# Cluster similarities by token: tokens as weights, centroids streamed, parts added by GpSimd, selection spread over four steps

## The chip, the core and the metric

The kernel runs on one core of one Trainium2 chip. TensorE (PE in the profile) does matrix products and writes them to PSUM; its weight loads have rows of their own (PEld). VectorE (DVE), ScalarE (ACT) and GpSimd (POOL) work element by element; SyncE (SP) issues nearly all DMAs. Every engine runs its own instructions in order and waits on semaphores. The metric is the device time of one execution in microseconds (us), lower is better; the time before is the median of three runs.

## The reference, cut to what matters

```
q_n, k_n, c_n = each row divided by its norm
q_assign = argmax(q_n @ c_n.T)      # 16 centroids a head, per token
k_assign = argmax(k_n @ c_n.T)
mask = q_assign[:, None] == k_assign[None, :]
scores = where(mask, scale * q @ k.T, -1e9)
attn = exp(scores - max) / (sum + 1e-9)
x = attn @ v                        # (2 batches x 768 tokens) x 512
h = x @ w_in;  x = (gelu-like of h) @ w_out
h = x @ w_in2; out = (relu(h) ** 2) @ w_out2
```

There are 2 batches, 8 heads, 768 tokens and 64 dimensions a head. The change touches the first three lines, the similarities to 16 centroids and the choice of the largest.

## The kernel before

**Tiles and groups.** Attention works in 8 groups of two heads. A group has 12 query tiles of 128 tokens, so there are 96 tiles in all (`NTILE`). Float32 values are held as two parts, `hi` and `lo` (k1 and k2 for the operand that stacks k in the upper and scaled q in the lower 64 partitions), so that products in the fast float32 format keep their precision.

**The loop.** The main loop runs over t from -2 to 95. A pass issues, in this order: the scores of tile t+2 and their row maximum (`scores`, `rowmax`); six transposes of the exponentials of tile t (`turn_e`, line 426), each half copied by ScalarE (`hi_e`, 436) and its remainder formed by VectorE (`lo_e`, 439); then "mid" and "ahead" side work; a share of the product with the values (`av`, 451; `AV_CUTS` says how many of the 12 matmuls of a block of three tiles fall into each pass); the exponential of tile t+2 (`expo`, 417); and the rest of the side work. Call u = (t+2) mod 12 the step. At step 0 the scores of a new group begin; during steps 0 to 11 the side work prepares the next group. What `side` hands out at each step sets the order; no scheduler moves anything.

**Similarities.** At steps 3 and 4 `sims` takes the centroids `cpad` as weights and streams 384 tokens: four matmuls a step (two heads, k1 and k2). The result has one row per centroid, head and part, so it lies transposed. `simmed` (295) copies it out; at step 5 `best` turns it back with six plain float32 matmuls against a doubled identity, `ident2`, which also adds the two parts (301), into the PSUM bank `pm`.

**Selection.** Still at step 5 `bested` has VectorE take the maximum over 16 and compare (307, 309), and GpSimd weight the hits so that the first one wins (312). At step 7 `hot` takes the maximum and compares again (318, 320), which gives one-hot rows `hot_n`. At step 8 `rows` turns these on TensorE (349), `rowed` has ScalarE turn them into mask values `oh` (359) and issues eight small DMAs (377) that put them under q1 and k1: four for the group's first head, then four for the second. The first scores of the group, at step 12 (step 0 of the next round), read them as 16 more rows of the product (402).

**Beginning and end.** Group 0 has a shorter form of the selection (`first_best`, `first_hot`), head by head on VectorE. After the last tile the first hidden chunk of the first layer is begun (138), in the bank `sd`. That bank was used just before for the last group's sums (`recip_rows`, 485 and 487).

Of the kernel before, what the change touches and what calls it, by code (L numbers as in the profile page):

```python
# [29 lines left out]
def f32(ap):  # L30
    return ap.bitcast(F32)
# [3 lines left out]
def tile_kernel(ctx, tc, q, k, v, cent, w_in1, w_out1, w_in2, w_out2, cw_cols, out):  # L35
# [107 lines left out]
    def attention(actx):  # L143
# [53 lines left out]
        cpad = one.tile([P, H, 2, NS * C], F32R, name="cpad")  # L197
# [13 lines left out]

        ident2 = one.tile([P, NS * C], F32, name="ident2")
        nc.vector.tensor_copy(ident2[0:NS * C], identF[0:NS * C, 0:NS * C])
        nc.vector.tensor_copy(ident2[NS * C:], identF[NS * C:, NS * C:])
# [20 lines left out]
        def centroid_columns(c_hl):  # L235
# [4 lines left out]
            for x in range(2):  # L240
                of = slice(D * (1 - x), D * (2 - x))
                for i in range(G):
                    o = C * (x * G + i)
                    nc.scalar.copy(cpad[of, i::G, :, o:o + C].rearrange("p h t c -> p t h c"),
                                   f32(pc[of, :, i::G, :]))


        class Prep:
# [43 lines left out]
            def simmed(self, half):  # L292
                if half == 0:
                    self.st = one.tile([P, S], F32, tag="st", name="st")
                nc.scalar.copy(self.st[:, half * QB:(half + 1) * QB], self.ps)

            def best(self):

                self.pm = psum([P, NJ, NS, C], F32, "sd", "pm")
                for j in range(NJ):  # L300
                    nc.tensor.matmul(self.pm[:, j].rearrange("p h c -> p (h c)"),  # L301
                                     self.st[:, j * P:(j + 1) * P], ident2, start=True, stop=True)

            def bested(self):
                pm = self.pm
                mx = tiny.tile([P, NJ, NS], F32, tag="mx", name="mx", bufs=1)
                nc.vector.tensor_reduce(out=mx, in_=pm, op=ALU.max, axis=AX)
                sim = one.tile([P, NJ, NS, C], F32, tag="sim", name="sim")
# [3 lines left out]
                nc.gpsimd.tensor_tensor(  # L312
                    out=self.simw.rearrange("p j h c -> p (j h) c"), in0=sim.rearrange("p j h c -> p (j h) c"),
                    in1=cwf.unsqueeze(1).to_broadcast([P, NJ * NS, C]), op=ALU.mult)

            def hot(self):
                fi = tiny.tile([P, NJ, NS], F32, tag="fi", name="fi", bufs=1)
                nc.vector.tensor_reduce(out=fi, in_=self.simw, op=ALU.max, axis=AX)
# [4 lines left out]
            def first_best(self, hh):  # L323

                if not hh:
                    self.sim = one.tile([P, NJ, NS, C], F32, tag="sim", name="sim")
# [3 lines left out]
                pm, sim = self.pm[:, :, hh::G], self.sim[:, :, hh::G]  # L330
                mx = tiny.tile([P, NJ, G], F32, tag="mx1", name="mx", bufs=1)
                nc.vector.tensor_reduce(out=mx, in_=pm, op=ALU.max, axis=AX)
                nc.vector.tensor_tensor(
                    out=sim, in0=pm, in1=mx.unsqueeze(3).to_broadcast([P, NJ, G, C]), op=ALU.is_equal)
# [776 lines left out]
```

## Time and profile before

| | us |
|---|---|
| median of 3 runs | 774.65 (773.09 to 775.04) |
| the profiled execution | 772.62 |
| its span, first to last instruction | 770.8 |
| PE busy | 758.3 (98%) |
| DVE busy | 600.2 (78%) |
| ACT busy | 502.1 (65%) |
| POOL busy | 132.5 (17%) |

The span is 1.8 us shorter than the execution's own time. Attention takes roughly the first third of it, up to 250 us; the two layers take the rest. A busy share tells little about a single stage: what counts is which engine ends last in a step, and that is read in the timelines.

### The profile page before, as it was taken

How to read it: one execution, taken by the hardware profiler on the slowest of the kernel's cores; microseconds unless marked ns; L12 is line 12 of the kernel's file. 1: busy time of each engine (PE TensorE's matmuls, PEld its weight loads, DVE VectorE, ACT ScalarE, POOL GpSimd, SP SyncE). 2: the span in 40 equal slices, each digit the busy share in tenths (PEclk: the TensorE clock that was granted, in tenths of full speed). 3: DMA queues.
4: the chain of work that ended last, by engine and by line, in shares of the span. 5: the costliest groups of instructions: out<-in, count | busy, mean ns of one | idle time of the engine just before them, and what ended most of it. 6: DMA issues, size and time to landing. Idle time of an engine off the chain costs nothing.

```text
span 770.8 us, 12158 instructions
## 1 busy us (share of the span) xinstructions
PE 758.3 (98%) x4400; PEld 694.4 (90%) x4401; DVE 600.2 (78%) x1087; ACT 502.1 (65%) x1035; POOL 132.5 (17%) x151
## 2 busy tenths in 40 slices
PE   7999999999999999999999999999999999999998
PEld 4899999999998899999899999999998888888886
DVE  5899999988898776888888877898778896454532
ACT  5798898898898654544665655576555666445442
POOL 0465474474565100000000000000000000000000
PEclk9999999999999999999999999999999999999999
DMA  9855845734510555445444343314333303100002
GB/s 217 198 122 131 203 106 144 184 90 119 122 42 22 158 172 169 138 151 192 137 149 153 95 129 114 126 45 148 114 121 96 110 28 122 43 28 28 28 1 82
DMA packets 71740, 88.14 MB, mean 114 GB/s; under 512 B 30432, under 2 KB 53760, under 8 KB 71680
## 3 DMA queue, kind: packets, MB, share of 16 engines
q1 hardware_dynamic: 69824, 86.94, 39.4%
q8 instruction: 34, 0.56, 0.3%
q10 hardware_dynamic: 1856, 0.43, 0.3%
q14 instruction: 26, 0.21, 0.1%
HBM read 58.76 MB, written 11.58 MB: 91 GB/s over the span
## 4 chain that ended last, share of the span: by engine, by line
PE 91%; DVE 4%; ACT 1%; DMA 1%; POOL 1%; issue 1%; ACTq 0%; SPq 0%; DVEq 0%; POOLq 0%
PE ps L839 22%; PE y L733 16%; PE y L727 11%; PE pa L451 9%; PE pt L426 8%; PE y L729 6%; PE ph L138 4%; PE ps L402 4%; PE ps L403 4%; PE ps L138 3%; PE pm L301 1%; PE ps L289 1%; PE pt L257 1%; DMA rawkq<-in_q_dram 1%; DVE xl L782 1%
## 5 line engine op out<-in xcount | busy, mean ns | idle before, releaser
L710 ACT ACTIVATE gh<-h 128x384 fp32r<-128x384 f32 (+1 forms) x64 | 41.4, 647 | 101.1 <-DVE h L700 71.2
L408 DVE TENSOR_REDUCE nm<-ps 128x1 f32<-128x768 f32 x96 | 91.6, 954 | 16.6 <-PE ps L403 15.7
L439 DVE TENSOR_TENSOR el<-pt,eh 128x384 fp32r<-128x384 f32 x192 | 97.4, 548 | 5.6 <-ACT eh L436 4.3
L436 ACT CAST eh<-pt 128x384 fp32r<-128x384 f32 x192 | 83.5, 490 | 16.4 <-PE pt L426 16.1
L417 ACT ACTIVATE e<-ps,nm 128x768 f32<-128x768 f32 x96 | 88.1, 917 | 5.8 <-DVE nm L408 5.7
L714 DVE TENSOR_TENSOR gl<-h,gh 128x384 fp32r<-128x384 f32 (+1 forms) x104 | 68.4, 660 | 19.6 <-ACT h L711 19.5
L426 PE MATMUL pt<-identF,e 128*128 128x128 f32 x576 | 80.0, 274 | 0.4 <-DVE el L439 0.4
L733 PE MATMUL y<-ol,gh 128*128 128x512 f32 x192 | 75.9, 395 | 0.1
L733 PE MATMUL y<-oh,gl 128*128 128x512 f32 x192 | 75.9, 395 | 0.0
L733 PE MATMUL y<-oh,gh 128*128 128x512 f32 x192 | 74.7, 389 | 0.0
L402 PE MATMUL ps<-k,q 80*128 80x512 f32 x192 | 69.5, 362 | 0.8 <-ACT k L369 0.8
L426 PEld LDWEIGHTS pt<-identF,e 128*128 128x128 f32 x576 | 65.2, 141 | 2.7 <-DVE el L439 1.9
L403 PE MATMUL ps<-k,q 128*128 128x512 f32 x192 | 62.1, 344 | 0.0
L809 DVE TENSOR_TENSOR wxl<-wb,wxh 128x512 fp32r<-128x512 f32 x37 | 25.6, 691 | 40.7 <-ACT wxh L808 40.7
L727 PE MATMUL y<-gh,ol 128*128 128x512 f32 x128 | 50.0, 391 | 0.0
L727 PE MATMUL y<-gh,oh 128*128 128x512 f32 x128 | 50.0, 391 | 0.0
L727 PE MATMUL y<-gl,oh 128*128 128x512 f32 x128 | 50.0, 391 | 0.0
L839 PE MATMUL ps<-xh,wxh 128*128 128x384 f32 x192 | 48.9, 335 | 0.7 <-DVE h L700 0.7
L839 PE MATMUL ps<-xl,wxh 128*128 128x384 f32 x192 | 49.1, 337 | 0.0
L839 PE MATMUL ps<-xh,wxl 128*128 128x384 f32 x192 | 49.1, 336 | 0.0
L451 PE MATMUL pa<-eh,v 128*128 128x384 f32 x192 | 47.3, 361 | 0.0
L451 PE MATMUL pa<-el,v 128*128 128x384 f32 x192 | 46.6, 352 | 0.0
(198 smaller groups left out, 1882.8 us busy)
## 6 DMA issues: line engine op xcount, KB each, us to landing
raw<-in_moe_w_in_dram SPq DMA_DIRECT2D x32, 512.0 KB, 4.0
raw<-in_moe_w_out_dram SPq DMA_DIRECT2D x32, 512.0 KB, 3.6
wb<-wst SPq DMA_DIRECT2D x24, 512.0 KB, 3.4
q<-k SPq DMA_DIRECT2D x48, 192.0 KB, 3.2
wst<-room SPq DMA_DIRECT2D x16, 256.0 KB, 2.2
wst<-wb SPq DMA_DIRECT2D x13, 256.0 KB, 2.3
rawkq<-in_k_dram SPq DMA_DIRECT2D x16, 192.0 KB, 3.9
k<-k SPq DMA_DIRECT2D x16, 192.0 KB, 5.2
```

What stands on the lines that cost most here:

```text
L402: nc.tensor.matmul(ps[:, a:a + n], q1[0:K1, qs], k1[0:K1, a:a + n], start=True, stop=False)
L403: nc.tensor.matmul(ps[:, a:a + n], q2[:, qs], k2[:, a:a + n], start=False, stop=True)
L408: nc.vector.tensor_reduce(out=nm, in_=live["s", t][:, 0:S], op=ALU.max, axis=AX, negate=True)
L417: nc.scalar.activation(e, live["s", t][:, 0:S], ACTF.Exp, bias=live.pop(("nm", t)), accum_out=sums[:, s:s + 1])
L426: nc.tensor.transpose(pt[:, i], e[:, kc * P:(kc + 1) * P], identF)
L436: nc.scalar.copy(place("eh", t, u), live["pt", t, u])
L439: nc.vector.tensor_tensor(out=place("el", t, u), in0=live.pop(("pt", t, u)), in1=f32(place("eh", t, u)), op=ALU.subtract)
L451: nc.tensor.matmul(pa, v2[:, i % NJ, :], src[:, i % NJ, :], start=(i == 0), stop=(i == 2 * NJ - 1))
L714: nc.vector.tensor_sub(g[1][:, at], h[:, c, at], f32(g[0][:, at]))
L727: nc.tensor.matmul(y[m], l[:, cs], r[:, 0:512], start=first, stop=last)
L733: nc.tensor.matmul(y[m], l[:, m * P:(m + 1) * P], r, start=(begin and z == 0), stop=(fc == KF - 1 and z == 2))
L839: nc.tensor.matmul(ps, w[a][:, wi, kc * P:(kc + 1) * P], x[z][kc], start=start and j == kc == 0, stop=j == 2 and kc == 1, skip_group_check ...
```

## The change

It does seven things.

1. Similarities by token: 128 tokens are the weights and 64 columns of centroids are streamed, so a token's similarities land in its own row. A group has 24 matmuls of 64 columns, 12 at step 3 and 12 at step 4, in the place of 8 of 384 columns; the six plain float32 matmuls and `ident2` are gone. `cpad` is half as wide.
2. The two parts, from the upper and the lower partitions, are added by GpSimd: one addition of 192 elements a partition behind each copy (group 0: by VectorE, from PSUM and a copied part).
3. The selection is one VectorE operation a step: `best` at 5, `bested` at 6, `first` at 7, `hot` at 8. `rows` and `rowed` move from step 8 to step 9.
4. `TURNS`: one of the four transposes of the group after next moves from step 9 to step 8. `AV_CUTS`: four value matmuls a step in three of four blocks.
5. Group 0: its similarities go into the large bank `big0`, so that bank `sd` is free; GpSimd prepares the values of the second head after the splits of group 1 instead of before.
6. The last sums are turned in the spare part of a score bank (`live["s", NTILE - 1]`), not in `sd`.
7. The first hidden chunk: 4 of its 12 matmuls go ahead of the transposes of tile 94, the other 8 ahead of the last value product.

```diff
-            def sims(self, half, tag="sd"):
-                self.ps = psum([P, QB], F32, tag, "ps")
-                cols = slice(half * QB, (half + 1) * QB)
-                both = [(n, hh) for hh in range(G) for n in ("k1", "k2")]
-                for x in both:
-                    nc.tensor.matmul(self.ps, cpad[:, self.h0 + x[1]].rearrange("p t c -> p (t c)"),
-                                     self.__dict__[x][:, cols], start=(x == both[0]), stop=(x == both[-1]))
+            def sims(self, tiles, heads=range(G), ps=None):
+                self.ps = psum([P, NQ, 2, 2, G, C], F32, "sd", "ps") if ps is None else ps
+                for hh in heads:
+                    for i, j in enumerate(tiles):
+                        for n in ("k1", "k2"):
+                            nc.tensor.matmul(self.ps[:, i, :, :, hh], self.__dict__[n, hh][:, j * P:(j + 1) * P],
+                                             cpad[:, self.h0 + hh], start=(n == "k1"), stop=(n == "k2"))
...
-                nc.scalar.copy(self.st[:, half * QB:(half + 1) * QB], self.ps)
+                nc.scalar.copy(st, self.ps.rearrange("p j t x g c -> p j t (x g) c"))
+                nc.gpsimd.tensor_tensor(out=self.sim[:, tiles[0]:tiles[-1] + 1], in0=st[:, :, 0], in1=st[:, :, 1],
+                                        op=ALU.add)
...
-                self.pm = psum([P, NJ, NS, C], F32, "sd", "pm")
-                for j in range(NJ):
-                    nc.tensor.matmul(self.pm[:, j].rearrange("p h c -> p (h c)"),
-                                     self.st[:, j * P:(j + 1) * P], ident2, start=True, stop=True)
+                self.mx = tiny.tile([P, NJ, NS], F32, tag="mx", name="mx", bufs=1)
+                nc.vector.tensor_reduce(out=self.mx, in_=self.sim, op=ALU.max, axis=AX)
...
-                    out=sim, in0=pm, in1=mx.unsqueeze(3).to_broadcast([P, NJ, NS, C]), op=ALU.is_equal)
+                    out=self.sim, in0=self.sim, in1=mx.unsqueeze(3).to_broadcast([P, NJ, NS, C]), op=ALU.is_equal)
...
-            pr = live["s", t][0:GT, S:S + P] if t < NTILE else psum([GT, P], F32, "sd", "pr")
+            pr = live["s", min(t, NTILE - 1)][0:GT, S:S + P]
...
-        AV_CUTS = ((0, 3, 7, 12), (0, 5, 8, 12), (0, 4, 8, 12), (0, 6, 9, 12))
+        AV_CUTS = ((0, 4, 8, 12), (0, 4, 8, 12), (0, 4, 8, 12), (0, 6, 9, 12))
...
-        TURNS = (-5, -3, -1, 0)
+        TURNS = (-5, -4, -1, 0)
...
-            elif u == 8:
-                pe, copy = p.rows, p.rowed
-            if u == 5:
-                ahead, copy = p.best, p.bested
-            if u == 7:
-                mid = p.hot
+            if u == 9:
+                pe.append(p.rows)
+                copy.append(p.rowed)
+            for on, fn in ((5, p.best), (6, p.bested), (7, p.first), (8, p.hot)):
+                if u == on:
+                    mid.append(fn)
...
+            if t == NTILE - 2:
+                first = [hidden(xs, w1, 0, span=slice(0, KD))]
...
-        first = [hidden(xs, w1, 0, span=slice(0, KD))]
+        hidden(xs, w1, 0, first[0], slice(KD, 3 * KD))
...
-        hidden(xs, w1, 0, first[0], slice(KD, 3 * KD))
```

Three places show how the order moves. The first is ScalarE at steps 7 to 9 of the first round, ahead of group 1; `e` is an exponential, `full` the copy for a split, `eh` a copied half of transposes and `oh` the mask values. Before:

```order
L267 ACTIVATE full_582<-pt_574,kq_scale_142 128x384
L436 CAST eh_597<-pt_593 128x3x128
L436 CAST eh_597<-pt_601 128x3x128
L417 ACTIVATE e_613,sums_352<-ps_586,nm_591 128x768
L359 ACTIVATE oh_622<-pf_618,mscale_147 128x384
L436 CAST eh_597<-pt_639 128x3x128
L436 CAST eh_597<-pt_645 128x3x128
L417 ACTIVATE e_654,sums_352<-ps_632,nm_637 128x768
L267 ACTIVATE full_663<-pt_659,kq_scale_142 128x384
```

The same place of ScalarE now:

```order
L260 ACTIVATE full_596<-pt_588,kq_scale_142 128x384
L433 CAST eh_611<-pt_607 128x3x128
L433 CAST eh_611<-pt_615 128x3x128
L414 ACTIVATE e_628,sums_357<-ps_600,nm_605 128x768
L260 ACTIVATE full_637<-pt_633,kq_scale_142 128x384
L433 CAST eh_611<-pt_648 128x3x128
L433 CAST eh_611<-pt_654 128x3x128
L414 ACTIVATE e_664,sums_357<-ps_641,nm_646 128x768
L356 ACTIVATE oh_673<-pf_669,mscale_147 128x384
```

The mask values `oh` and the second `full` have changed places: `oh` comes one exponential later.

The second place is VectorE at steps 5 to 8 of the same round; `mx` and `fi` are the two maxima, `nm` a row maximum of scores and `el` a remainder. Before:

```order
L307 TENSOR_REDUCE mx_510<-pm_495 128x24
L309 TENSOR_TENSOR sim_512<-pm_495,mx_510 128x384
L408 TENSOR_REDUCE nm_521<-ps_516 128x1
L439 TENSOR_TENSOR el_486<-pt_523,eh_485 128x3x128
L439 TENSOR_TENSOR el_486<-pt_529,eh_485 128x3x128
L408 TENSOR_REDUCE nm_546<-ps_541 128x1
L439 TENSOR_TENSOR el_486<-pt_548,eh_485 128x3x128
L439 TENSOR_TENSOR el_486<-pt_554,eh_485 128x3x128
L318 TENSOR_REDUCE fi_560<-simw_514 128x24
L320 TENSOR_TENSOR hot_n_562<-simw_514,fi_560 128x384
L408 TENSOR_REDUCE nm_591<-ps_586 128x1
```

The same place of VectorE now, from the second operation of the selection on:

```order
L300 TENSOR_TENSOR sim_459<-sim_459,mx_519 128x384
L405 TENSOR_REDUCE nm_563<-ps_558 128x1
L436 TENSOR_TENSOR el_510<-pt_565,eh_509 128x3x128
L436 TENSOR_TENSOR el_510<-pt_571,eh_509 128x3x128
L309 TENSOR_REDUCE fi_577<-simw_550 128x24
L405 TENSOR_REDUCE nm_605<-ps_600 128x1
L436 TENSOR_TENSOR el_612<-pt_607,eh_611 128x3x128
L436 TENSOR_TENSOR el_612<-pt_615,eh_611 128x3x128
L314 TENSOR_TENSOR hot_n_621<-simw_550,fi_577 128x384
L405 TENSOR_REDUCE nm_646<-ps_641 128x1
```

Two pairs have become four single operations, and the last of them stands one row maximum later.

The third place is TensorE at the end of attention; `pr` and the last `ps` are the turned sums, `ph` the first hidden chunk. Before:

```order
L451 MATMUL pa<-eh,v_3344 128x384 x4
L426 MATMUL pt<-identF,e 128x128 x6
L451 MATMUL pa<-eh,v_3344 128x384 x2
L451 MATMUL pa<-el,v_3344 128x384 x6
L426 MATMUL pt<-identF,e 128x128 x6
L485 MATMUL pr<-identF,sums 12x128
L138 MATMUL ph<-xh,wi 128x384 x4
L451 MATMUL pa<-eh,v_3344 128x384 x6
L451 MATMUL pa<-el,v_3344 128x384 x6
L138 MATMUL ph<-xl,wi 128x384 x4
```

The same place of TensorE now:

```order
L448 MATMUL pa<-eh,v_3412 128x384 x4
L138 MATMUL ph<-xh,wi 128x384 x4
L423 MATMUL pt<-identF,e 128x128 x6
L448 MATMUL pa<-eh,v_3412 128x384 x2
L448 MATMUL pa<-el,v_3412 128x384 x6
L423 MATMUL pt<-identF,e 128x128 x6
L482 MATMUL ps<-identF,sums 12x128
L138 MATMUL ph<-xl,wi 128x384 x4
L138 MATMUL ph<-xh,wi 128x384 x4
L448 MATMUL pa<-eh,v_3412 128x384 x6
```

Four matmuls of the hidden chunk moved ahead of the transposes of tile 94 and eight ahead of the last value product.

## Rows read from the trace of the kernel before

**Rows 1.** The page: busy time by engine; the chain that ended last, by engine.

```profile
PE 758.3 (98%) x4400; PEld 694.4 (90%) x4401; DVE 600.2 (78%) x1087; ACT 502.1 (65%) x1035; POOL 132.5 (17%) x151
PE 91%; DVE 4%; ACT 1%; DMA 1%; POOL 1%; issue 1%; ACTq 0%; SPq 0%; DVEq 0%; POOLq 0%
```

**Rows 2.** Timeline, TensorE, steps 4 and 5: start, length, line, tiles, count.

```profile
27.89 0.94 PE L289 MATMUL ps<-k,cpad 128*128 128x384 f32 x4
28.67 0.40 PE L402 MATMUL ps<-k,q 80*128 80x512 f32 x1
...
29.15 0.28 PE L402 MATMUL ps<-k,q 80*128 80x256 f32 x1
29.27 0.28 PE L403 MATMUL ps<-k,q 128*128 128x256 f32 x1
29.39 0.82 PE L426 MATMUL pt<-identF,e 128*128 128x128 f32 x6
30.05 1.52 PE L301 MATMUL pm<-ident,st 128*128 128x64 f32 x12
31.38 0.78 PE L451 MATMUL pa<-eh,v 128*128 128x384 f32 x3
```

**Rows 3.** Timeline, TensorE, a later round, end of step 8 to step 12.

```profile
68.42 0.34 PE L349 MATMUL pf<-identB,hot_n 128*128 128x128 bf16 x3
68.58 0.48 PE L402 MATMUL ps<-k,q 80*128 80x512 f32 x1
...
70.79 0.48 PE L402 MATMUL ps<-k,q 80*128 80x512 f32 x1
...
72.93 0.39 PE L402 MATMUL ps<-k,q 80*128 80x512 f32 x1
...
75.25 0.48 PE L402 MATMUL ps<-k,q 80*128 80x512 f32 x1
```

**Rows 4.** Timeline, ScalarE, the same round, steps 8 and 9.

```profile
69.44 0.71 ACT L359 ACTIVATE oh<-pf,mscale 128x384 fp32r<-128x384 bf16 x1
...
71.61 0.65 ACT L267 ACTIVATE full<-pt,kq_scale 128x384 f32<-128x384 f32 x1
```

**Rows 5.** Timeline, SyncE's queue, the same round.

```profile
70.17 1.34 SPq L377 DMA_DIRECT2D q<-oh  x2
71.56 1.22 SPq L377 DMA_DIRECT2D k<-oh  x2
```

**Rows 6.** The one-hot DMAs of that round (line 377): issue to landing.

```profile
DMA to landing us min/median/max: 1.9/1.9/1.9
```

**Rows 7.** Timeline, VectorE, the same round, steps 7 to 9.

```profile
66.90 0.56 DVE L320 TENSOR_TENSOR hot_n<-simw,fi 128x384 bf16<-128x384 f32 x1
...
68.34 1.02 DVE L439 TENSOR_TENSOR el<-pt,eh 128x384 fp32r<-128x384 f32 x2
69.57 0.96 DVE L408 TENSOR_REDUCE nm<-ps 128x1 f32<-128x768 f32 x1 [0.20 <-PE ps L403]
```

**Rows 8.** Timeline, GpSimd, the same round.

```profile
68.59 1.02 POOL L269 TENSOR_TENSOR k<-full,k 128x384 fp32r<-128x384 f32 x1
69.69 1.01 POOL L474 TENSOR_TENSOR x<-both 64x384 f32<-64x384 f32 x1
```

**Rows 9.** Timeline, VectorE and GpSimd around 85 us.

```profile
85.29 1.01 POOL L474 TENSOR_TENSOR x<-both 64x384 f32<-64x384 f32 x1 [2.87 <-DMA both<-both]
85.40 1.45 DVE L100 SCALAR_TENSOR_TENSOR raw<-raw,raw 128x512 uint32<-128x512 uint32 x1
```

**Rows 10.** VectorE's line 100 in attention: duration ns min/median/max, first and last start.

```profile
L100 DVE SCALAR_TENSOR_TENSOR raw<-raw,raw x4: 674/1109/1450, 56.0 to 144.6; 128x512 uint32<-128x512 uint32 x4
```

**Rows 11.** Timeline, TensorE and ScalarE, end of attention.

```profile
247.66 1.01 PE L426 MATMUL pt<-identF,e 128*128 128x128 f32 x6 [0.41 <-DVE el L439]
...
251.88 0.25 ACT L487 COPY rows<-pr 12x128 f32<-12x128 f32 x1
...
252.27 0.93 PE L138 MATMUL ph<-xh,wi 128*128 128x384 f32 x4 [1.44 <-POOL x L474]
```

**Rows 12.** Timeline, TensorE, group 0: its one-hot rows are turned.

```profile
15.78 0.34 PE L349 MATMUL pf<-identB,hot_n 128*128 128x128 bf16 x3 [1.01 <-DVE sim L333]
```

More of the change, by code (lines that the diff above doesn't have):

```diff
@@ L196, in attention @@
         nc.vector.memset(kq_scale[D:], SCALE)
-        cpad = one.tile([P, H, 2, NS * C], F32R, name="cpad")
+        cpad = one.tile([P, H, 2, 2, C], F32R, name="cpad")
         nc.vector.memset(f32(cpad), 0.0)
@@ L241, in centroid_columns @@
                 of = slice(D * (1 - x), D * (2 - x))
[L242 to L245, printed above, removed]
+                nc.scalar.copy(cpad[of, :, :, x].rearrange("p h t c -> p t h c"), f32(pc[of]))
         class Prep:
@@ new lines, in simmed @@
+            def simmed(self, tiles):
+                if not tiles[0]:
+                    self.st = one.tile([P, NJ, 2, NS, C], F32, tag="st", name="st")
+                    self.sim = one.tile([P, NJ, NS, C], F32, tag="sim", name="sim")
+                st = self.st[:, tiles[0]:tiles[-1] + 1]
+                nc.scalar.copy(st, self.ps.rearrange("p j t x g c -> p j t (x g) c"))
+                nc.gpsimd.tensor_tensor(out=self.sim[:, tiles[0]:tiles[-1] + 1], in0=st[:, :, 0], in1=st[:, :, 1],
+                                        op=ALU.add)
@@ L306, in bested @@
[L306 to L308 removed]
+                mx = self.mx
                 nc.vector.tensor_tensor(
[L310 removed]
+                    out=self.sim, in0=self.sim, in1=mx.unsqueeze(3).to_broadcast([P, NJ, NS, C]), op=ALU.is_equal)
@@ L325, in first_best @@
                 if not hh:
+                    self.st = one.tile([P, NJ, 2, NS, C], F32, tag="st", name="st")
                     self.sim = one.tile([P, NJ, NS, C], F32, tag="sim", name="sim")
@@ L519, in attention @@
         w1 = (wi[:, 0, :], wi[:, 1, :]) + out_tiles(0)
-        for half in range(2):
-            p0.sims(half, ("sd", "pa")[half])
-            p0.simmed(half)
+        p0.sims(range(NJ), ps=psum([P, 8, 2, 2, G, C], F32, "big0", "ps"))
         nc.scalar.activation(tiny.tile([P, 1], F32, name="warm", bufs=1), identF[:, 0:1], ACTF.Exp)
@@ L528, in attention @@
         raw = [w_dma(w_in1, 0, True, 0), w_dma(w_out1, 0, False, 1)]
-        p0.best()
         p0.first_best(0)
         p0.first_hot(0)
-        for i in range(2):
-            p0.vals(i)
+        p0.vals(0)
         tags = iter(("pt0", "pt1", "pa", "big1"))
@@ L550, in attention @@
         dec = raw_tile(2).rearrange("p n t -> p (n t)")
-        none = lambda: None
-        TURNS = (-5, -3, -1, 0)
+        TURNS = (-5, -4, -1, 0)
         def side(gn, u):
-            mid = ahead = spare = pe = copy = none
+            mid, spare, pe, copy = [], [], [], []
             if not 0 < gn < NG:
-                return mid, ahead, spare, pe, copy
+                return mid, spare, pe, copy
             p = ops.get(gn) or Prep(gn)
@@ L563, in side @@
                 hh, half = divmod(TURNS.index(u), 2)
[L564 to L578 removed]
+                pe.append(lambda: p.turn(hh, half))
+                copy.append(lambda: p.split(hh, half))
+            if u in (3, 4):
+                at = range((u - 3) * NQ, (u - 3 + 1) * NQ)
+                pe.append(lambda: p.sims(at))
+                copy.append(lambda: p.simmed(at))
+            if u == 9:
[4 more added lines that the diff above has]
+                    mid.append(fn)
+            if u in (-2, 1) and gn > 1 or gn == 1 and u in (2, 3):
+                spare.append(lambda: p.moved(u in (1, 3)))
+            if u in (8, 8 + 1):
+                spare.append(lambda: p.vals(u - 8))
+            if u == 4 + 1:
+                spare.append(lambda: [p.joined(hh) for hh in range(G)])
             if u in (1, 2, 3) and gn + 1 < NG:
                 load(gn + 1, (0, 1, "v")[u - 1])
[L581 removed]
+            return mid, spare, pe, copy
         for t in range(-LEAD, NTILE):
@@ L601, in attention @@
             for fns in now:
-                fns[0]()
-            for fns in now:
-                fns[1]()
+                for fn in fns[0]:
+                    fn()
             if blk > 0 and t < NTILE - 1:
@@ L617, in attention @@
                 expo(t + LEAD)
-            for fns in list(zip(*now))[2:]:
-                for fn in fns:
+            for part_fns in list(zip(*now))[1:]:
+                for fn in sum(part_fns, []):
                     fn()
```

37 lines of the change are left out of this document (13 added, 24 removed).

## The prediction

> **What bounds the kernel.** I read the page first: TensorE is busy 758.3 of 770.8 us, and 91% of the chain that ended last is TensorE's [rows 1]. Then the timelines of single steps, to see whether TensorE's order has holes that a change can fill or open. Inside attention there are almost none: matmul follows matmul. So a change there counts in two ways only: work taken off TensorE's order, and waits that open in it. Work moved between the other engines counts only where it makes TensorE wait. I write step u for the passes of one round, 0 to 11; step 12 is step 0 of the next round. Seven rounds prepare a group (groups 1 to 7); group 0 is prepared ahead of the loop.
>
> **1. The similarity matmuls.** Before, a group has 4 matmuls of 384 columns at step 3 and 4 at step 4. The four at step 4 take from 27.89 to the next start at 28.67, 0.78 us [rows 2]. The six plain float32 matmuls at step 5 have two records each: 12 records from 30.05 to 31.38, 1.33 us, 0.111 each [rows 2]. A group costs 2 x 0.78 + 1.33 = 2.89 us. After, it has 24 matmuls, each with a new load of 128 x 128 weights and 64 columns. No row before shows this one. The nearest is the record of the six plain matmuls, with the same load size and the same 64 columns, at 0.111; the transposes with their 128 x 128 loads pace the same, six from 29.39 to 30.05, 0.11 each [rows 2]. That makes 24 x 0.111 = 2.66, a gain of 0.23 a group. From above: the shortest matmul of this number format has 256 columns and takes 0.12, from 29.15 to 29.27 [rows 2]; if 64 columns are no cheaper, 24 x 0.12 = 2.88 and nothing is gained. From below: the three bf16 transposes take 68.58 - 68.42 = 0.16, 0.053 each [rows 3]; 24 x 0.053 = 1.28, a gain of 1.6. I stay with the row that has the same loads, halfway to the upper one: 0.12 a group, 8 x 0.12 = **-1.0**. The point is that the loads set the pace, so that streaming six times fewer columns frees almost nothing.
>
> A page of the Trainium skill says otherwise: TensorE: Matmul & The Clock Gate, section on the back-to-back issue gap, gives about 81 ns per pair of load and matmul at 128 columns. The trace shows 110 ns for such pairs with float32 weights [rows 2]. By the page a group would cost 1.94 us, the term would be -7.6, and the sum below 772.1 in place of 778.7; it is taken up as a rival, priced there from rows.
>
> **2. The mask rows come a step later.** This is the largest term. In the round shown, ScalarE starts the mask values at 69.44 and ends 0.71 later [rows 4]; the first DMAs issue at 70.17, the second pair at 71.56, so the fourth at about 72.17 [rows 5]; 1.9 us later it has landed [rows 6], at 74.1. The first scores of the new group start at 75.25 [rows 3]. They read the rows of the first head's q and of all its k, so they wait for the fourth DMA. Margin before: about 1.15 us. After, `rows` and `rowed` stand at step 9: the mask values take the place where ScalarE now does a split copy, at 71.61 [rows 4]. That is 2.17 later; TensorE's distance from there to step 12 does not grow (the step 9 that had three transposes has the three one-hot ones in their place, and steps 10 and 11 keep their four value matmuls). The fourth DMA then lands at about 76.25, **1.0 us after** TensorE needs it. Behind that one matmul queue all of TensorE's next scores, transposes and value products; VectorE and ScalarE only run dry, so nothing is won back. Bounds: 0.7, if part of the 1.9 is not waited for or TensorE is itself a little later; 1.3, if the mask values start later still (part 3). I take 0.95, seven times: **+6.6**.
>
> SyncE's other DMAs behind these eight (the merge copy, the q and k of the group after next) move 2 us too; their readers come three or more steps later, so I cost them at nothing; if that margin were gone, a step would wait as here.
>
> **3. One selection operation a step.** Same four operations, other places. VectorE's regular work in a step is 0.96 + 1.02 = 1.98 us, and it waits only 0.20 for the next scores [rows 7]; a step of TensorE with four value matmuls takes 72.93 - 70.79 = 2.14, and 2.32 with three transposes more [rows 3]. Each selection operation adds 0.56 [rows 7]. Steps 5 to 8 now need 4 x 2.54 = 10.2 us of VectorE against 2 x 2.14 + 2 x 2.32 = 8.9 of TensorE, since the six plain matmuls that made step 5 long are gone and steps 3 and 4 hold the similarity work. The 1.2 us of backlog is partly absorbed by the idle time before it and worked off in steps 9 to 11. What is left makes TensorE wait for a free transpose bank or a late exponential. On top, `hot` moves to a time when GpSimd is at work: before, it started at 66.90, ahead of GpSimd's 68.59 [rows 7, 8]; now it starts near 69.4, between 68.59 + 1.02 and an operation at 69.69 [rows 8]. A VectorE operation with two inputs in the main on-chip memory waits for a GpSimd one: line 100 takes 0.67 alone and 1.45 when it starts 0.11 after a GpSimd addition [rows 9, 10]. So `hot` can cost up to 0.8 more. Bounds a round: 0 (all absorbed) and 1.3. I take 0.4, the part of the backlog that steps 9 to 11 can't take: 7 x 0.4 = **+2.8**.
>
> **4. GpSimd's additions.** 14 of 192 elements, at most 1.0 each (the 384-element one takes 1.02 [rows 8]). ScalarE's copy ends early in step 5 and VectorE reaches the maximum only after its 1.98 of regular work, so they are covered; uncovered, up to 1 us a round. GpSimd is busy 17% [rows 1]. ScalarE's copies stay as long. Cost 0.
>
> **5. The end of attention.** TensorE waits 0.41 before the transposes of tile 94 and 1.44 before the hidden chunk [rows 11]. The second wait ends with ScalarE's copy of the turned sums, 251.88 + 0.25, since both use bank `sd` (the row names a GpSimd operation that ended at the same time; the chunk needs none that late). After, the sums lie in a score bank, four matmuls of the chunk fill the first wait and eight the second; a group of four takes 0.77 with its start-up, so both waits fill. What follows, ScalarE's split of the next weights, comes forward with the value product. **-1.9**, between -1.0 and -2.3.
>
> **6. Start.** The turn of group 0's one-hot rows waited 1.01 us for VectorE's second-head comparison, since both shared `sd` [rows 12]. That bank is now free, but one addition and one copy are new in the chain. I take **-0.4**, between -1.0 and +0.7.
>
> **Sum.** -1.0 + 6.6 + 2.8 - 1.9 - 0.4 = +6.1. Against the profiled execution's own 772.6 that gives 778.7; the median of the runs lies 2.0 above that execution, so the median after should be **780.7 us**.
>
> **Rivals.**
> - *The mask rows land in time, VectorE's backlog is absorbed.* Then only the gains remain: -1.0 - 1.9 - 0.4 = -3.3, **771.4 us, faster**. It decides where the fourth DMA's landing falls against the first score matmul of step 12: from a margin at or above zero there the kernel is faster. Against it: the move is a whole step of 2.17 and the margin 1.15. For it: I read the margin in one round, and only one execution.
> - *Half of it.* Waits at their lower ends, 7 x 0.7 = +4.9 and no backlog: +1.6, **776.2**, no difference that can be told.
> - *Loads pace faster than I read.* At the bf16 pace the gain is 1.6 a group, 12.9 in all in place of 1.0: 780.7 - 11.9 = **768.8**. For: the columns are few. Against: every pair with 128 x 128 float32 weights paces at 0.11. The skill's 81 ns lies between and would give 774.1.
> - *The small products cost two records each*, as the plain float32 ones do: 48 x 0.111 = 5.33 against 2.89, +2.4 a group, 8 x 2.4 = +19.5 in place of -1.0: **801**. Against: the 384-column ones of this format have one record each.
>
> **How the numbers follow.** A measurement of this kernel can tell about 0.3%, 2.3 us: faster is below 772.3, slower above 777.0. Forecast (mask rows late, 776.5 to 787 by the bounds of parts 2 and 3): 0.55, all slower. In time: 0.22, of which 0.18 faster, 0.04 same. Half of it: 0.12, of which 0.07 same, 0.04 slower, 0.01 faster. Faster loads: 0.08, of which 0.05 faster, 0.03 same. Two records: 0.03, slower. Sums: faster 0.24, same 0.14, slower 0.62. The range for 8 in 10 goes from 770.8, just below the in-time case, to 786.5; the forecast's own range is 776.5 to 787.
>
> **What would show it.** In the profile after: at step 12 of each round, the first score matmul with idle time of about 1 us released by a DMA of the mask rows, seven times, 6 to 7 us in all (part 2). At steps 6 to 9, transposes or scores waiting for VectorE's remainders, and `hot` longer than 0.56 beside GpSimd (part 3). The 24 small matmuls at 0.11 each, one record each (part 1). No wait of 1.44 before the hidden chunk (part 5). I am wrong if the step-12 matmuls show no DMA wait, or if the small matmuls pace well under 0.1.

## The result: 779.2 us, slower

| | before | after |
|---|---|---|
| median of the runs taken together, us | 773.87 (772.58 to 775.04, 4 runs) | 779.21 (778.95 to 779.37, 4 runs) |
| span of the profiled execution, us | 770.8 | 777.6 |
| PE busy, us | 758.3 | 758.7 |
| DVE busy, us | 600.2 | 597.9 |
| POOL busy, us | 132.5 | 141.8 |

The ratio is 1.0069, 95% interval 1.005 to 1.0088: slower by 5.3 us, where the forecast sum was +6.1. The time lies in the range and the sign is right. The sum behind it is less right: its largest term came out too small, and the second largest was not there at all.

The page of the changed kernel, busy time by engine and the chain that ended last by engine, answers to [rows 1]:

```profile
PE 758.7 (98%) x4432; PEld 693.8 (89%) x4433; DVE 597.9 (77%) x1087; ACT 504.6 (65%) x1033; POOL 141.8 (18%) x165
...
PE 83%; DVE 7%; ACT 4%; DMA 2%; issue 2%; SPq 1%; ACTq 0%; DVEq 0%
```

TensorE does as much as before in a span 6.8 us longer: the loss is waiting, and TensorE's share of the chain falls from 91% to 83%. What it waits for stands in the table of waits of the changed kernel (engine, waiting instruction, what released it: us in total, times, longest):

```profile
PE ps L399 <- DMA k<-oh: 5.5, 5, 1.5
PE ps L399 <- ACT full L260: 2.3, 2, 1.2
PE pt L423 <- DVE el L436: 0.2, 1, 0.2
```

Line 399 is the first score matmul, and the seven waits are those of step 12. One of them, in the timelines of TensorE, SyncE's queue and ScalarE, the round of [rows 3 to 5]:

```profile
73.97 0.39 PE L399 MATMUL ps<-k,q 80*128 80x512 f32 x1
...
75.34 0.94 PE L448 MATMUL pa<-eh,v 128*128 128x384 f32 x4
76.12 0.49 PE L250 MATMUL pt<-identF,rawkq 128*128 128x128 f32 x3
77.77 0.47 PE L399 MATMUL ps<-k,q 80*128 80x512 f32 x1 [1.16 <-ACT full L260]
```

```profile
73.58 1.34 SPq L374 DMA_DIRECT2D q<-oh  x2
74.97 1.22 SPq L374 DMA_DIRECT2D k<-oh  x2
```

```profile
72.89 0.66 ACT L356 ACTIVATE oh<-pf,mscale 128x384 fp32r<-128x384 bf16 x1
...
77.10 0.61 ACT L260 ACTIVATE full<-pt,kq_scale 128x384 f32<-128x384 f32 x1
```

The row puts this wait down to `full`, a ScalarE copy that happens to end at 77.71, but the first scores need nothing of it; the fourth mask DMA, issued at about 74.97 + 0.61 = 75.58, is 2.2 us old when TensorE goes on (the run kfirst below settles which of the two it is). Idle time in a row is counted from the modelled end of the last matmul. I count from first score matmul to first score matmul instead: step 11 lasts 77.77 - 73.97 = 3.80 here, and 75.25 - 72.93 = 2.32 before [rows 3], with the same instructions. In the seven rounds it lasts 3.63 to 3.79 (before 2.07 to 2.42), together **9.9 us** more.

The same reckoning for other steps shows where an experiment loses or gains, so it stands here once for all. Lengths of steps 5 to 11 in us, median of the seven rounds, each the distance between the starts of two first score matmuls:

| step | before | after | rows8 | hot7 | kfirst | pair5 | halves | oldcuts |
|---|---|---|---|---|---|---|---|---|
| 5 | 3.32 | 2.15 | 2.16 | 2.15 | 2.15 | 2.16 | 2.16 | 1.98 |
| 6 | 2.09 | 2.07 | 2.06 | 2.07 | 2.07 | 2.06 | 2.07 | 2.08 |
| 7 | 2.49 | 2.31 | 2.31 | 2.31 | 2.31 | 2.90 | 2.37 | 2.65 |
| 8 | 2.47 | 2.40 | 2.30 | 2.40 | 2.40 | 2.30 | 2.31 | 2.49 |
| 9 | 2.21 | 2.30 | 2.79 | 2.61 | 2.30 | 2.39 | 2.67 | 2.27 |
| 10 | 2.14 | 2.17 | 2.15 | 2.16 | 2.16 | 2.16 | 2.16 | 2.16 |
| 11 | 2.32 | 3.69 | 2.31 | 3.47 | 3.03 | 2.31 | 2.31 | 2.31 |

### The profile page after: what moved, and what is told of

Read it like the earlier page. It is cut to its first block, busy times and chain, and to the rows that moved or that the text cites. A ratio compares the mean times of both kernels' runs of the same rounds, so it can differ in the third digit from the quotient of the medians.

```text
span 777.6 us, 12239 instructions
## 1 busy us (share of the span) xinstructions
PE 758.7 (98%) x4432; PEld 693.8 (89%) x4433; DVE 597.9 (77%) x1087; ACT 504.6 (65%) x1033; POOL 141.8 (18%) x165
## 4 chain that ended last, share of the span: by engine, by line
PE 83%; DVE 7%; ACT 4%; DMA 2%; issue 2%; SPq 1%; ACTq 0%; DVEq 0%
PE ps L835 21%; PE y L729 16%; PE y L723 11%; PE pa L448 6%; PE pt L423 6%; PE y L725 6%; PE ph L138 4%; PE ps L399 4%; PE ps L138 3%; PE ps L400 3%; PE ps L282 2%; DVE el L436 1%; ACT e L414 1%; DVE nm L405 1%; DMA k<-oh 1%
## 5 line engine op out<-in xcount | busy, mean ns | idle before, releaser
L399 PEld LDWEIGHTS ps<-k,q 80*128 80x128 f32 x192 | 36.7, 191 | 15.5 <-ACT e L414 8.0
```

What stands on the lines that cost most here:

```text
L399: nc.tensor.matmul(ps[:, a:a + n], q1[0:K1, qs], k1[0:K1, a:a + n], start=True, stop=False)
```

## The experiments

Theory A: the loss is the wait for the mask DMAs and nothing else. Theory B: the similarities by token or the additions on GpSimd cost something. Theory C, from my forecast: one selection operation a step gives VectorE a backlog for which TensorE pays. Medians are compared with runs of the kernel before on the same chip, 772.9 us in each of the four sets that follow. The changed kernel was not run again in these sets (its own kernel before stood at 773.87), so a difference to it of about 1 us is read from the table of steps and not from the medians.

**rows8: the mask rows a step earlier again.**

```
-        TURNS = (-5, -4, -1, 0)
+        TURNS = (-5, -3, -1, 0)
-            if u == 9:
+            if u == 8:
                 pe.append(p.rows)
...
-            for on, fn in ((5, p.best), (6, p.bested), (7, p.first), (8, p.hot)):
+            for on, fn in ((5, p.best), (6, p.bested), (7, p.first), (7, p.hot)):
```

> The changed kernel with the mask rows (rows, rowed) back at step 8, the one-hot rows (hot) at step 7 behind first, and the four transposes of the group after next back at their old steps; everything else as changed. Theory A (the whole loss is TensorE waiting at step 12 for the fourth mask DMA): the seven waits, 8.9 us together in the changed kernel's trace, are gone, so 779.2 - 8.9 = 770.3 us, 3.6 below the kernel before (ratio 0.995), and no step-12 score matmul shows idle time. Theory B (the similarities by token or the additions on GpSimd cost something that the trace puts down to the mask rows): part of the 8.9 stays, 773 us or more. Theory C (my forecast's term for VectorE's backlog): two operations at step 7 make TensorE wait at steps 7 to 8, visible as idle time there.

771.46 us, ratio to the kernel before 0.9975 (0.9966 to 0.9984): 7.7 us less than the changed kernel. Step 11 is back at 2.31. The rest of the change, without the late mask rows, makes the kernel faster, so B, which asked for 773 or more, falls. But 1.2 us of the expected 8.9 are missing (9.9 by step 11), and the table shows where: step 9 lasts 2.79. It has the three float32 transposes now (71.30 - 71.06 = 0.24) where the changed kernel has the bf16 ones (0.15), which makes 2.39, and pair5 below, with the same matmuls in step 9 and no wait there, has just 2.39. The other 0.40 is a wait of the transposes, in two halves. TensorE's rows there and its weight loads' rows (PEld), which name the releaser:

```profile
69.19 0.28 PE L400 MATMUL ps<-k,q 128*128 128x256 f32 x1
69.50 0.31 PEld L423 LDWEIGHTS pt<-identF,e 128*128 128x128 f32 x3 [0.24 <-DVE el L436]
69.50 1.01 PE L423 MATMUL pt<-identF,e 128*128 128x128 f32 x6
69.96 0.31 PEld L423 LDWEIGHTS pt<-identF,e 128*128 128x128 f32 x3 [0.16 <-DVE el L436]
71.06 0.49 PE L250 MATMUL pt<-identF,rawkq 128*128 128x128 f32 x3
71.30 0.48 PE L399 MATMUL ps<-k,q 80*128 80x512 f32 x1
```

The transposes need a bank that VectorE's remainder `el` (line 436) has yet to read, and VectorE is late: `first` and `hot` stand in one step, behind a delay from steps 5 and 6 (the table under oldcuts).

**hot7: that pair alone.** The mask rows stay at step 9; only `hot` goes to step 7.

```
-            for on, fn in ((5, p.best), (6, p.bested), (7, p.first), (8, p.hot)):
+            for on, fn in ((5, p.best), (6, p.bested), (7, p.first), (7, p.hot)):
```

> The changed kernel with hot at step 7 behind first, ahead of GpSimd's operations, and the mask rows left at step 9. Theory A: hot is only a small part of why the mask values are late (it holds up the row maximum of step 9 and with it the exponential ahead of the mask values by about 0.1 us), so the seven waits fall by at most 0.15 each: 778.2 to 779.2 us. Theory C (one selection operation a step costs by itself, 0.4 us a round as forecast): 776.4 us.

780.23 us, 1.0 **slower** than the changed kernel. Both expectations missed, and C most of all. `hot` takes 0.56 there in place of 0.73, and the step-11 wait shrinks by 0.2 (3.69 to 3.47), but step 9 grows by 0.31 (2.30 to 2.61), again a wait of the transposes for `el`. The first score matmul of step 8 and VectorE's timeline of hot7:

```profile
67.38 0.48 PE L399 MATMUL ps<-k,q 80*128 80x512 f32 x1
68.17 0.54 DVE L309 TENSOR_REDUCE fi<-simw 128x24 f32<-128x384 f32 x1
68.74 0.56 DVE L314 TENSOR_TENSOR hot_n<-simw,fi 128x384 bf16<-128x384 f32 x1
69.22 0.95 DVE L405 TENSOR_REDUCE nm<-ps 128x1 f32<-128x768 f32 x1
70.08 1.01 DVE L436 TENSOR_TENSOR el<-pt,eh 128x384 fp32r<-128x384 f32 x2
```

The same step of the changed kernel:

```profile
67.11 0.48 PE L399 MATMUL ps<-k,q 80*128 80x512 f32 x1
68.34 0.95 DVE L405 TENSOR_REDUCE nm<-ps 128x1 f32<-128x768 f32 x1
```

The row maximum of step 8 starts 69.22 - 67.38 = 1.84 into its step, in the changed kernel 68.34 - 67.11 = 1.23: 0.61 later. So the pair is what costs here. One operation a step costs TensorE nothing: step 6 lasts 2.07 (before 2.09); step 7 is 0.18 shorter, which is the value matmul of 0.17 that left it; step 8, where a value matmul left and the three transposes grew from 0.16 to 0.25, is 0.07 shorter.

**kfirst: another order of the DMAs.**

```
                 for hh in heads:
-                    for x in range(2):
-                        for z in range(2):
-                            dst, src = piece(x, hh, z)
-                            nc.sync.dma_start(f32(dst), f32(src))
+                    for x, z in ((0, 0), (1, 0), (1, 1), (0, 1)):
+                        dst, src = piece(x, hh, z)
+                        nc.sync.dma_start(f32(dst), f32(src))
```

> The changed kernel with one thing moved: of the four DMAs of a head, the two for k stand ahead of the second one for q, which only the odd query tiles read. Nothing moves on TensorE, ScalarE or VectorE. Theory A: the last DMA that step 12 needs is now the third, issued 0.63 us earlier, so each of the seven waits falls from 1.28 to about 0.65 us: 779.2 - 4.4 = 774.8 us. If the wait is for something else (the score bank, ScalarE's copy that ends at the same time in the record): 779.2, no change.

774.53 us, ratio 1.0019 (1.001 to 1.0027): 4.7 less than the changed kernel, 4.4 expected. Step 11 falls by 0.66 to 3.03. No compute engine's order moved, so this is the run that shows theory A: TensorE waits for the last DMA that its first score matmul reads. TensorE and SyncE's queue:

```profile
74.41 0.49 PE L250 MATMUL pt<-identF,rawkq 128*128 128x128 f32 x3
75.27 0.47 PE L398 MATMUL ps<-k,q 80*128 80x512 f32 x1 [0.36 <-issue]
```

```profile
71.87 0.67 SPq L373 DMA_DIRECT2D q<-oh  x1
72.59 1.25 SPq L373 DMA_DIRECT2D k<-oh  x2
```

The third DMA, the second of k's, issues at about 73.2, and TensorE starts 2.0 to 2.1 later, as it does behind the fourth in the changed kernel.

**tailback: the end of attention as before.**

```
-            pr = live["s", min(t, NTILE - 1)][0:GT, S:S + P]
+            pr = live["s", t][0:GT, S:S + P] if t < NTILE else psum([GT, P], F32, "sd", "pr")
...
-            if t == NTILE - 2:
-                first = [hidden(xs, w1, 0, span=slice(0, KD))]
...
-        hidden(xs, w1, 0, first[0], slice(KD, 3 * KD))
+        first = [hidden(xs, w1, 0, span=slice(0, KD))]
...
         merged(blk, nc.vector)
+        hidden(xs, w1, 0, first[0], slice(KD, 3 * KD))
```

> The changed kernel with the end of attention as before: the last sums turned in bank sd, the first hidden chunk begun behind the turned sums. Theory: the end's two waits of 0.41 and 1.44 come back, 779.2 + 1.9 to 2.3 = 781.1 to 781.5 us. Rival (the next stage absorbs it, so that the change's gain at the end is not real): 779.2.

781.5 us, 2.3 more than the changed kernel. The two waits of [rows 11] come back at the same size, 0.41 and 1.44. The gain at the end is real, and nothing after it takes it back.

**before_rows9: the move alone, in the old kernel.**

```
-        TURNS = (-5, -3, -1, 0)
+        TURNS = (-5, -4, -1, 0)
...
-            elif u == 8:
+            elif u == 9:
                 pe, copy = p.rows, p.rowed
```

> The kernel before with one part of the change alone: the mask rows (rows, rowed) at step 9 and, to free their bank, the transpose of the group after next from step 9 to step 8. Old similarities, selection in pairs, old end. Theory A: in the trace of before the first scores start 3.05 us after the fourth mask DMA's issue; in the changed kernel they could not start earlier than 2.0 to 2.15 after it; a step of 2.2 later leaves 0.85 of distance, so each of seven rounds waits about 1.2: +8.4, 773.0 + 8.4 = 781.4 us. Theory B (the new similarities or GpSimd's additions make the changed kernel's waits): no change, 773 us.

783.27 us, ratio 1.0131 (1.0116 to 1.0146): 10.3 more than before, 8.4 expected. The waits of step 12 are there without any of the new similarities. TensorE, one of them:

```profile
78.61 0.49 PE L257 MATMUL pt<-identF,rawkq 128*128 128x128 f32 x3
80.11 0.47 PE L402 MATMUL ps<-k,q 80*128 80x512 f32 x1 [1.01 <-DMA k<-oh]
```

Step 11 is 9.1 us longer in seven rounds together. The remaining 1.2 was not followed further; in the profiled execution group 1's similarities also wait 1.3 us for GpSimd's splits.

**pair5: the pair at another step.** On top of rows8:

```
-            for on, fn in ((5, p.best), (6, p.bested), (7, p.first), (7, p.hot)):
+            for on, fn in ((5, p.best), (5, p.bested), (6, p.first), (7, p.hot)):
```

> The changed kernel with the mask rows at step 8 (as in the run with rows and rowed back at step 8), and the selection one step earlier instead of a pair at step 7: best and bested at step 5, first at 6, hot at 7. Theory: the run with the pair at step 7 has a wait of 0.2 us a round, TensorE's transposes of step 9 waiting for a remainder of VectorE, 1.4 us in seven rounds; at step 5 VectorE has just stood idle for the two long similarity steps, so the pair costs nothing there: 771.5 - 1.4 = 770.1 us, with no wait at all in the seven rounds. Rival (the pair costs the same wherever it stands): 771.5, with waits at step 6 or 7.

773.1 us, 1.6 more than rows8 and no better than the kernel before (1.0002, 0.9993 to 1.0011). My theory falls: the idle time that VectorE had ahead of step 5 is no use to a pair at step 5, since the pair comes behind that step's row maximum and remainders. Step 7 grows from 2.31 to 2.90 and step 9 gives back 0.40, 0.2 a round net. TensorE's timeline:

```profile
64.06 0.28 PE L400 MATMUL ps<-k,q 128*128 128x256 f32 x1
64.56 1.01 PE L423 MATMUL pt<-identF,e 128*128 128x128 f32 x6 [0.23 <-DVE el L436]
```

**halves: the selection in halves**, begun at step 4, so that step 7 holds half of `first` beside `hot` (on top of rows8; `best`, `bested` and `first` take a half z of three tiles):

```
...
+            for on, fn, z in ((4, p.best, 0), (5, p.best, 1), (5, p.bested, 0), (6, p.bested, 1), (6, p.first, 0),
+                              (7, p.first, 1)):
+                if u == on:
+                    mid.append(lambda fn=fn, z=z: fn(z))
+            if u == 7:
+                mid.append(p.hot)
...
```

> The changed kernel with the mask rows at step 8, the one-hot rows at step 7 and the transposes at their old steps (as the run with rows and rowed back at step 8), and the selection's first three operations cut in halves of three tiles each, begun a step earlier: maximum of the first half at step 4; maximum of the second and comparison of the first half at 5; comparison of the second and first-hit maximum of the first at 6; first-hit maximum of the second half and the whole hot at 7. Theory (a step holds one VectorE operation of 0.56 more without loss; what exceeds it makes TensorE's transposes wait for a free bank): step 7 now has 0.3 + 0.56 in place of 1.12 and the wait of 0.2 a round shrinks to nothing: 771.5 - 1.4 = 770.1 us. Rival (small operations cost nearly as much as whole ones, and GpSimd's two half products collide with VectorE's): 771.5 or more.

772.4 us, 0.9 more than rows8. Step 9 falls by 0.12, but steps 7 and 8 grow by 0.07 together, so six rounds gain little. In the trace a half operation of three tiles takes 0.33 to 0.35 us (one `bested` half 0.50), where a whole one takes 0.54 to 0.56, so two halves cost VectorE more than the whole. The seventh round loses 1 us: `hot` runs into a long GpSimd operation. GpSimd, VectorE and TensorE there:

```profile
215.22 1.83 POOL L505 TENSOR_TENSOR x<-x,rr 128x768 f32<-128x768 f32 x1
```

```profile
215.72 1.75 DVE L320 TENSOR_TENSOR hot_n<-simw,fi 128x384 bf16<-128x384 f32 x1
```

```profile
217.52 0.34 PE L352 MATMUL pf<-identB,hot_n 128*128 128x128 bf16 x3 [0.80 <-DVE hot_n L320]
```

**oldcuts: the old shares of the value product.** On top of rows8:

```
-        AV_CUTS = ((0, 4, 8, 12), (0, 4, 8, 12), (0, 4, 8, 12), (0, 6, 9, 12))
+        AV_CUTS = ((0, 3, 7, 12), (0, 5, 8, 12), (0, 4, 8, 12), (0, 6, 9, 12))
```

> The changed kernel with the mask rows at step 8 and the pair first, hot at step 7 (as the run with rows and rowed back at step 8), and the old shares of the value product: five matmuls at steps 7 and 8 in place of four, fewer at steps 5 and 9. Theory: the pair at step 7 costs 0.3 us a round only because steps 7 and 8 are 0.17 shorter each on TensorE than in the kernel before, where the same pair at step 7 cost nothing; with the old shares VectorE has that time back, and the step-9 wait goes: 771.5 - 7 x 0.3 = 769.4 us. Rival (the wait comes from elsewhere, as from GpSimd's and ScalarE's order at step 8): 771.5.

771.13 us, ratio 0.9973 (0.9962 to 0.9984), not told apart from rows8: 0.3 less, 2.1 expected. Step 9 falls to 2.27, by 0.17 for the matmul that moved and by 0.35 for the wait; step 7 grows by 0.34, twice the 0.17 of the matmul that came. Half of the wait has only moved forward by two steps.

Why the kernel before bears its pair at step 7 can be read from VectorE's timelines. From the start of one row maximum to the next, VectorE needs 1.80 to 1.85 us in a step without a selection operation (where it has no idle time), 2.26 with one and 2.85 with two. Here are the row maxima of steps 6 to 8 of the changed kernel, then those of steps 7 and 8, with the pair in between, of the kernel before and of rows8:

```profile
63.83 0.95 DVE L405 TENSOR_REDUCE nm<-ps 128x1 f32<-128x768 f32 x1
...
66.09 0.95 DVE L405 TENSOR_REDUCE nm<-ps 128x1 f32<-128x768 f32 x1
...
68.34 0.95 DVE L405 TENSOR_REDUCE nm<-ps 128x1 f32<-128x768 f32 x1
```

```profile
64.52 0.96 DVE L408 TENSOR_REDUCE nm<-ps 128x1 f32<-128x768 f32 x1 [0.18 <-PE ps L403]
...
67.38 0.95 DVE L408 TENSOR_REDUCE nm<-ps 128x1 f32<-128x768 f32 x1
```

```profile
65.19 0.95 DVE L405 TENSOR_REDUCE nm<-ps 128x1 f32<-128x768 f32 x1
...
68.03 0.95 DVE L405 TENSOR_REDUCE nm<-ps 128x1 f32<-128x768 f32 x1
```

The pair costs VectorE the same in both; what differs is how long the step is and how late VectorE already is. The table gives the start of the row maximum behind the start of its step's last score matmul (us, median of six rounds; 0.32 where VectorE has been waiting for the scores). A wait of TensorE in the next step, if there is one, stands in brackets:

| step | before | after | rows8 | pair5 | oldcuts |
|---|---|---|---|---|---|
| 6 | 0.32 | 0.51 | 0.52 | 1.11 (0.59) | 0.69 (0.17) |
| 7 | 0.32 | 0.70 | 0.71 | 1.30 | 0.88 |
| 8 | 0.60 | 0.56 | 1.16 (0.40) | 0.57 | 0.99 (0.05) |
| 9 | 0.32 | 0.77 | 0.65 | 0.32 | 0.32 |

Before, step 6 holds no operation and step 7 lasts 2.49, so the pair starts on time and leaves VectorE 0.28 late, which TensorE does not notice. With one operation in each of steps 5 and 6, the pair comes on top of 0.39 (rows8, where step 7 lasts 2.31) or 0.56 (oldcuts). In pair5 the pair starts on time, but its step lasts only 2.16, and VectorE is 0.79 late behind it. No run changes the delay ahead of the pair alone.

**rows8_kfirst: a control.** rows8 with the DMA order of kfirst.

> A control: the changed kernel with the mask rows at step 8, and k's mask DMAs ahead of q's second one. Theory: where the fourth DMA is in time, its place costs nothing and gains nothing: the same as with the rows at step 8 alone, 771.5 us.

771.09 us (0.9975, 0.9964 to 0.9986), the same as rows8: where nothing waits for the DMA, its place is worth nothing.

**rows10: the mask rows later still.**

```
-            if u == 9:
+            if u == 10:
                 pe.append(p.rows)
```

> The changed kernel with the mask rows one step later still, at step 10. Theory A: each of the seven waits at step 12 grows by the length of a step, 2.15 to 2.2 us: 779.2 + 7 x 2.2 = 794.5 us. Rival (ScalarE's order absorbs part of it, since no split copy stands at step 10): less than 790.

824.5 us, 45 more than the changed kernel, not 15. Step 11 lasts 8.7 in the middle rounds. The mask values end on ScalarE at 81.51 + 0.67 = 82.2, but their DMAs now stand in SyncE's order behind three that move the next group's q (line 271), and those issue from 82.94 on:

```profile
82.94 1.74 SPq L271 DMA_DIRECT2D q<-k  x3
84.79 1.42 SPq L374 DMA_DIRECT2D q<-oh  x2
```

So a step of 2.2 is paid, and then 2.6 more in the queue. Step 0 behind the wait lasts 4.33 in the place of 2.38, and the seven together 13.4 us more: that is TensorE's clock, in the last section.

**halfcols: half the columns**, in groups 1 to 7. It leaves out the product with the low part of the centroids.

```
+                            out, c = self.ps[:, i, :, :, hh], cpad[:, self.h0 + hh]
+                            if self.gi:
+                                out, c = self.ps[:, i, 0, :, hh], cpad[:, self.h0 + hh, 0]
-                            nc.tensor.matmul(self.ps[:, i, :, :, hh], self.__dict__[n, hh][:, j * P:(j + 1) * P],
-                                             cpad[:, self.h0 + hh], start=(n == "k1"), stop=(n == "k2"))
+                            nc.tensor.matmul(out, self.__dict__[n, hh][:, j * P:(j + 1) * P],
+                                             c, start=(n == "k1"), stop=(n == "k2"))
...
```

> The changed kernel with half the columns in the 24 small matmuls of groups 1 to 7: 32 in place of 64. It leaves out the product with the low part of the centroids. In the trace of the changed kernel 24 of them take 2.51 us a group, 0.105 each. Theory (the weight loads set their pace): 32 columns pace the same, 2.5 us a group. Rival (the columns count): the pace falls towards half, 1.3 us a group.

779.61 us in one run. TensorE in the changed kernel, and in halfcols:

```profile
25.70 1.51 PE L282 MATMUL ps<-cpad,k 128*128 128x64 f32 x12
27.04 0.48 PE L399 MATMUL ps<-k,q 80*128 80x512 f32 x1
```

```profile
25.42 1.49 PE L285 MATMUL ps<-cpad,k 128*128 128x32 f32 x12
26.76 0.48 PE L402 MATMUL ps<-k,q 80*128 80x512 f32 x1
```

Twelve take 1.34 us with 64 columns and 1.34 with 32: 0.112 each. Between 32 and 64 the columns do not count. What the two have in common is a new load of 128 x 128 float32 weights for every matmul; that this load sets the pace fits the float32 transposes (0.11 with the same loads [rows 2]), but no run changes the loads alone.

## Why the prediction was right, and where it was not

The sum, term by term, in us:

| step of the prediction | forecast | measured | by |
|---|---|---|---|
| 1. similarity matmuls | -1.0 | about -1.0 | steps 3 to 5, timelines |
| 2. mask rows a step later | +6.6 | +9.9 | step 11; kfirst, rows8, before_rows9 |
| 3. one selection operation a step | +2.8 | about 0 | steps 6 to 10 |
| 4. GpSimd's additions | 0 | about 0 | VectorE's timeline, rows8 |
| 5. end of attention | -1.9 | -2.3 | tailback |
| 6. start | -0.4 | not resolved | first scores at 17.69, before 17.74 |
| sum | +6.1 | +6.6 | spans of the profiles: +6.8 |

*Part 1, right.* 0.112 a matmul is the row of the six plain matmuls [rows 2] almost exactly. Steps 3 to 5 of group 6, which nothing disturbs, last 185.67 - 177.14 = 8.53 after and 8.49 before; one value matmul of 0.17 came to step 5, so the similarities gain 0.13 a group, 1.0 in eight, where 0.12 a group was forecast. The Trainium skill, TensorE: Matmul & The Clock Gate, section on the back-to-back issue gap, has 81 ns for a pair at 128 columns; here pairs take 112 ns at 64 and at 32 columns, and the measurement decides. The rivals with faster loads and with two records each fall: a group has 24 records.

*Part 2, right in its mechanism, its size too small.* 1.4 a round, above the upper end of 1.3. Two terms were short. First, I counted 1.9 from issue to landing [rows 6], but TensorE goes on 2.01 to 2.17 after the fourth issue in all seven rounds: the landing that the profile shows is not yet the start of the one that waits. Second, I moved the mask values by one step of 2.17; they come a little later in their step (72.89 is 1.08 after the first scores of step 10, while 69.44 was 0.86 after those of step 9 [rows 3, 4]). VectorE's timeline shows one reason: `hot` is slowed beside GpSimd to 0.73, and the row maximum behind it holds up the exponential that stands ahead of the mask values:

```profile
70.30 0.73 DVE L314 TENSOR_TENSOR hot_n<-simw,fi 128x384 bf16<-128x384 f32 x1
70.95 0.94 DVE L405 TENSOR_REDUCE nm<-ps 128x1 f32<-128x768 f32 x1
```

```profile
71.99 0.90 ACT L414 ACTIVATE e<-ps,nm 128x768 f32<-128x768 f32 x1 [0.17 <-DVE nm L405]
```

So a piece of what I had put down under part 3 as a wait of TensorE's own ended up inside part 2. hot7 shows its size: with `hot` out of the way the wait falls by 0.2.

*Part 3, wrong.* This is the step that failed: "Steps 5 to 8 now need 4 x 2.54 = 10.2 us of VectorE", and with it "What is left makes TensorE wait". I added the durations of the rows, 0.96 + 1.02 + 0.56. Rows that follow each other on VectorE overlap by nearly 0.1 each: from row maximum to row maximum a step with one operation takes 2.26, and 2.61 where `hot` is slowed. That is 9.4 in four steps against TensorE's 8.9, so VectorE is 0.45 late at step 9 and not 1.2. TensorE waits for none of it, and step 9, without an operation, works it off: the row maximum of step 10 is back at 0.32. A pair, at 2.85, is too much for a step of 2.16 to 2.31: by the table of steps hot7 loses 0.31 a round at step 9, and pair5 0.59 at step 7. The spreading that I booked as a cost is, on the new similarities, a gain against the pair.

*Part 5, right*, with 2.3 at the upper end of its bounds, more than the two waits of 1.85 together. *Part 4, right*: VectorE goes from its remainders to `best` without idle time. *Part 6* can't be told: the first scores start anywhere from 17.69 to 20.10 in the traces of runs whose beginning is the same. *The rival in which the mask rows land in time* gave 771.4, from the other terms alone; rows8, where they do, came out at 771.46, with a different cost in it, the pair. That the forecast time was only 1.5 us off is partly luck: two errors of opposite sign, 3.3 too little in part 2 and 2.8 too much in part 3, nearly cancel. Of the 1.5, 0.8 lies in the time before (774.65 when I forecast, 773.87 with one run more). The range was also added up wrong: the bounds of parts 2 and 3 give 776.2 to 789.4, not 776.5 to 787; the result lies in both.

The version to keep is rows8 with or without the other DMA order: 771.1 to 771.5 us, 0.25% below the kernel before.

## What to carry to other kernels

When a producer is moved a step later, measure its distance to the consumer from the start of the DMA's issue to the consumer's actual start in a run where it waits, and look at the order of the DMAs: putting the one that is needed first ahead was worth 4.7 us here where it was late, without moving any instruction of a compute engine, and nothing where it was in time. For small operations beside a tight pipeline, follow from step to step how late the engine is, and take its need from start to start and not from the sum of durations: one operation a step kept VectorE close to TensorE's pace, while two in one step cost TensorE time in a short step and none in a longer one that VectorE entered on time. Two errors can make a right total, so check the terms, not only the time.

## What the runs showed of the hardware

*In rows10 TensorE's waits of 3.8 to 6.2 us cost it its clock; in the changed kernel those of 1.0 to 1.5 us do not.* In rows10, TensorE's timeline and the table of stretches (us, then PE, PEld, DVE, ACT, POOL busy, granted clock, DMA share, GB/s) around one wait:

```profile
88.96 0.77 PE L399 MATMUL ps<-k,q 80*128 80x512 f32 x1 [6.15 <-DMA k<-oh]
89.52 0.63 PE L400 MATMUL ps<-k,q 128*128 128x512 f32 x1
```

```profile
82.50:88.90 6.40, 0.31 (x3) 0.07 (x1) 1.02 (x2) 1.79 (x5) 4.24 (x6) 0.83 0.48 109
88.90:92.90 4.00, 3.94 (x14) 3.72 (x15) 2.00 (x4) 1.48 (x3) 0.00 (x0) 0.50 0.33 76
```

and the changed kernel with its seven waits:

```profile
26.00:254.00 228.00, 220.20 (x1537) 205.36 (x1537) 197.65 (x333) 197.37 (x455) 129.50 (x146) 1.00 0.49 117
```

The clock is at 0.50, the 1.2 GHz level, for the 4 us behind the long wait: the 512-column score matmul at 89.52 takes 0.43 to the next start (89.95), and at the full clock 0.23 (74.21 to 74.44). The other six waits of rows10 are each followed by several us at 0.50 too. Seven such stretches of 4 us would bring the mean of the changed kernel's 228 us to 0.94; it is 1.00, so its waits cost their own length and no more.

*VectorE's `hot` and GpSimd's operations hold each other up.* `hot`, with two inputs in main on-chip memory, takes 0.56 alone. It takes 0.73 where it starts 0.70 into a GpSimd subtraction of 1.02, and 1.75 where it starts 0.50 into a GpSimd product of 1.83 (halves). In both it ends about 0.4 after the GpSimd operation does. In rows8 it starts 0.02 ahead of that same product: `hot` takes 0.56 and the product 2.23. The GpSimd row of the changed kernel, ahead of `hot` at 70.30:

```profile
69.60 1.02 POOL L262 TENSOR_TENSOR k<-full,k 128x384 fp32r<-128x384 f32 x1
```

The Trainium skill, SBUF — State Buffer, section Who interferes with whom and the one on the two separate sides, describes such a lock: whichever starts first keeps the shared ports for its whole instruction. The trace agrees in who is held up and for about how long.
